# Attention and GELU layers in one kernel: x by token blocks, half of the first weights ahead of step 3's v, copies moved to ScalarE, one last store per queue

## Chip, cores, metric

One core of one Trainium2 chip (trn2). The metric is device time in microseconds (us), the median of several executions of the whole kernel. In the profiles PE is TensorE (matmuls), PEld its weight loads, DVE VectorE, ACT ScalarE, POOL GpSimd, and SP the engine that issues most transfers. Profile times count from the start of the span, which is about 2 us shorter than the device time.

## The reference

A linear attention with decay over 768 tokens in blocks of 64, for 4 sequences and 8 heads of 64, then a two-layer network with GELU on its output:

```python
intra = np.einsum('bhic,bhjc->bhij', qb, kb) * Dmask[None]
intra = np.einsum('bhij,bhjd->bhid', intra, vb)
inter = np.einsum('bhid,bhde->bhie', qb * lam_pow[None], kv_state)
out[:, :, sl] = intra + inter
kv_state = lam_block * kv_state + np.einsum('bhsd,bhse->bhde', kb_dec, vb)
# ... (cut) x = out as 3072 tokens x 512
h = x @ w_in                       # 512 x 2048
g = 0.5 * h * (1.0 + np.tanh(c * (h + 0.044715 * h * h * h)))
return g @ w_out                   # 2048 x 512
```

## The kernel before

Attention runs in 24 steps, each 256 tokens of half of the heads. A step loads q, k, v, scales them by decays (`prep`), transposes q and k (`stage_t`, called transpose n below), computes scores, masks them (`causal`), multiplies by v and by the running state (`products`), copies the result to `xT`, and updates the state (`update`: t on VectorE, u on GpSimd). Groups of 256 or 512 tokens then go through the two layers: weight blocks (`mm1`, GELU on ScalarE) and output parts (`mm2`, copied out and stored). These are kept in a list, and `fill(n)` puts n of them between attention work so that PE is never idle. For the first group the matmuls begin before x is complete.

The parts that the change touches (cut):

```python
for nm, src in (("q", q), ("k", k), ("v", v)):          # load_step(s)
    ...
for s in range(4):
    load_step(s)
for j in range(4):
    load_win(j, 2 if j == 0 else 1)                     # first weights, in two halves
# ...
if s == 2:                                              # stage_t: PSUM -> SBUF
    for hp in range(2):
        nc.scalar.activation(out=o[:, :, :, hp, :], in_=Tps[:, :, :, hp, :], func=AF.Copy)
elif s in (1, 3):
    nc.scalar.activation(out=o[:], in_=Tps[:], func=AF.Copy)
else:
    nc.vector.tensor_copy(out=o[:], in_=Tps[:])
# ...
xT[g] = xtp.tile([P, NC, len(groups[g]) * SB], FP16, ...)            # products
dst = xT[g][:, 2 * half : 2 * half + 2, i * SB : (i + 1) * SB]
# ...
def mm1_begin(f, cs):                                   # first group, before x is complete
    for c in cs:
        w = N if c < 2 else SB
        nc.tensor.matmul(first[f][:, 0:w], w_in16[:, c, f * P : (f + 1) * P], x[:, c, 0:w], ...)
# ...
for lo, hi in ((0, 384), (384, DM)):                    # the last 128 rows of the output
    # 16 matmuls, then
    nc.vector.tensor_copy(out=o32[:, lo:hi], in_=o2[:])
    for j, eng in ((0, nc.sync), (1, nc.scalar)):
        eng.dma_start(out=dst[half64(j), lo:hi], in_=o32[half64(j), lo:hi])
# ... program order, steps 1 to 3
causal(1)
update(1, 0)
update(1, 1, "t")
idle(1)
stage_t(2)
idle(3)
prep(3)
```

## Time and profile before

| | before |
|---|---|
| device time, median (range), three runs | 214.52 us (214.45 to 214.91) |
| span of the profiled run | 212.4 us, granted clock 0.996 |
| PE busy | 203.6 us, 96% |
| waits of PE after its first start | about 3 us, all before 47 us |

The page, the waits of PE and its seams are shown in the prediction below. Two more places: first, the stretch of time around transpose 2, all engines. The columns are start, duration, engine, line, operation, result and operand, count, and in brackets how long the engine had been idle and what ended that:

```profile
12.15 1.09 ACT L230 ACTIVATE qkT<-Tps 128x512 f16<-128x512 f16 x2
12.49 0.27 DVE L347 COPY t<-OK 128x128 f32<-128x128 f32 x1
...
12.88 0.61 POOL L357 TENSOR_TENSOR u<-t,lumask 128x256 f16<-128x256 f32 x1
...
13.45 1.04 POOL L204 TENSOR_TENSOR qk<-q,dq 128x512 f16<-128x512 f32 x1
...
14.56 0.62 PE L225 MATMUL Tps<-ident,qk 128*128 128x128 f16 x8 [0.40 <-POOL qk L204]
```

One sees a chain: VectorE's state t, GpSimd's u, GpSimd's q of step 3, and transpose 3 on PE waiting for that q.

Second, the end (time line, 208 us on; SPq and ACTq are issues of transfers):

```profile
208.06 1.19 SPq L416 DMA_DIRECT2D out_dram<-o  x2
208.06 1.47 ACTq L416 DMA_DIRECT2D out_dram<-o  x2
208.37 0.29 DVE L414 COPY o<-O2ps 128x128 f32<-128x128 f32 x1 [0.34 <-PE O2ps L411]
```

Each queue issues two stores of 64 partitions. The two issues that follow the last copy start at 208.74 and take 0.51 and 0.79 us. From the end of that copy (208.66) to the end of the span (212.4) it is 3.74 us; I call this the tail.

### The profile page before, as it was taken

The page shows a single profiled execution, that of the slowest core. Times are in us where ns is not written, and L with a number is a line of the kernel's source. Part 1 is how long each engine was busy: PE and PEld are TensorE (multiplying, and loading weights), DVE is VectorE, ACT ScalarE, POOL GpSimd, SP SyncE. Part 2 cuts the span into 40 slices and gives each one's busy share as a digit, 9 for nine tenths or more (in the row PEclk, how much of TensorE's full clock was granted, in tenths as well). Part 3 has the DMA queues.
Part 4 walks back from the last instruction along what each step waited for, and adds up shares of the span by engine and source line. Part 5 has one row for each costly group of instructions (what it writes and reads, how often), then busy time and mean ns, then how long its engine had stood idle before and what let it go on. Part 6 is the DMA issues. An engine that isn't in the chain of part 4 may idle for free.

```text
span 212.4 us, 5060 instructions
## 1 busy us (share of the span) xinstructions
PE 203.6 (96%) x2121; PEld 107.2 (50%) x2121; DVE 88.3 (42%) x178; ACT 94.2 (44%) x177; POOL 65.7 (31%) x82
## 2 busy tenths in 40 slices
PE   7887999989999999999999999999999999999992
PEld 2454544446865874444455455444455454444451
DVE  4885520399885623540552441452431241100111
ACT  2484764325761661677320677320666111565000
POOL 5593135356583233422412320422420110000000
PEclk9999999999999999999999999999999999999998
DMA  5999999999999999973768373714120021100122
GB/s 134 300 329 385 387 386 361 284 292 328 306 259 195 316 216 251 240 191 67 191 199 214 134 197 69 182 72 130 49 54 0 3 89 59 52 0 0 49 96 54
DMA packets 61895, 37.82 MB, mean 178 GB/s; under 512 B 17712, under 2 KB 54832, under 8 KB 61872
## 3 DMA queue, kind: packets, MB, share of 16 engines
q1 hardware_dynamic: 61712, 37.37, 63.7%
q8 instruction: 16, 0.26, 0.5%
q10 hardware_dynamic: 160, 0.13, 0.2%
q14 instruction: 7, 0.06, 0.1%
HBM read 27.27 MB, written 6.29 MB: 158 GB/s over the span
## 4 chain that ended last, share of the span: by engine, by line
PE 87%; SPq 4%; DMA 3%; DVE 3%; issue 0%; ACT 0%
PE Hps L380 37%; PE O2ps L391 36%; SPq L67 4%; DMA wi<-in_moe_w_in_dram 3%; PE Sps L255 3%; PE OK L319 3%; PE OK L310 2%; PE O2ps L411 2%; PE Hps L426 1%; PE OK L296 1%; PE Tps L225 1%; DVE o L398 1%; DVE qkT L235 1%; DVE PT L272 1%; PE Hps L432 0%
## 5 line engine op out<-in xcount | busy, mean ns | idle before, releaser
L391 PE MATMUL O2ps<-w_out,gT 128*128 128x512 f16 x368 | 83.0, 379 | 0.0
L380 PE MATMUL Hps<-xT,w_in 128*128 128x512 f16 (+1 forms) x432 | 82.5, 347 | 0.0
L382 ACT ACTIVATE gT<-Hps 128x512 f16<-128x512 f32 x92 | 54.8, 597 | 27.4 <-PE Hps L380 26.7
L380 PEld LDWEIGHTS <-w_in 128*128 128x128 f16 x432 | 41.8, 98 | 36.0
L357 POOL TENSOR_TENSOR u<-t,lumask 128x256 f16<-128x256 f32 x40 | 29.0, 732 | 90.2 <-DVE t L350 67.2
L391 PEld LDWEIGHTS <-gT 128*128 128x128 f16 x368 | 35.3, 98 | 39.5
L272 DVE TENSOR_TENSOR PT<-Sps,mask 128x1024 f16<-128x1024 f32 (+1 forms) x25 | 29.4, 1179 | 51.7 <-PE Sps L255 51.6
L327 ACT ACTIVATE xT<-OK 128x256 f16<-128x256 f32 x48 | 18.4, 452 | 56.6 <-PE OK L319 44.0
L398 DVE COPY o<-O2ps 128x512 f32<-128x512 f32 x23 | 15.8, 690 | 44.6 <-PE O2ps L391 44.5
L194 POOL TENSOR_TENSOR v<-v,dv 128x512 f16<-128x512 f32 x24 | 26.7, 1116 | 5.6 <-DMA v<-in_v_dram 3.9
L204 DVE TENSOR_TENSOR qk<-q,dq 128x512 f16<-128x512 f32 x23 | 18.0, 783 | 10.7 <-DMA q<-in_q_dram 10.6
L209 ACT ACTIVATE qk<-k 128x512 f16<-128x512 f32 x24 | 15.0, 624 | 10.5 <-DMA k<-in_k_dram 10.5
L350 DVE SCALAR_TENSOR_TENSOR t<-t,lamu,OK 128x64 f32<-128x64 f32 x64 | 14.6, 274 | 1.9 <-issue 1.1
L255 PEld LDWEIGHTS <-qkT 64*64 64x64 f16 x384 | 6.2, 106 | 10.9 <-issue 6.6
L255 PE MATMUL Sps<-qkT 64*64 64x128 f16 x384 | 10.2, 222 | 1.2 <-DVE qkT L235 0.8
L310 PE MATMUL OK<-PT,v 64*64 64x128 f16 x384 | 10.2, 218 | 0.0
L462 PE MATMUL idle<-ones 128*128 128x512 f16 x25 | 8.6, 486 | 1.5 <-DVE ones L127 1.5
L108 POOL CAST w_out<-wo 128x1024 f16<-128x1024 f32 x6 | 6.1, 1040 | 10.3 <-DMA wo<-in_moe_w_out_dram 10.3
L319 PE MATMUL OK<-qkT,u 128*128 128x128 f16 x80 | 8.8, 222 | 0.1
L310 PEld LDWEIGHTS <-v 64*64 64x64 f16 x384 | 6.7, 108 | 1.3 <-issue 1.3
L98 DVE CAST w_in<-wi 128x1024 f16<-128x1024 f32 (+1 forms) x9 | 5.5, 654 | 3.8 <-DMA wi<-in_moe_w_in_dram 3.8
L296 PE MATMUL OK<-v,qk 64*64 64x64 f16 x320 | 7.0, 192 | 0.0
(41 smaller groups left out, 60.8 us busy)
## 6 DMA issues: line engine op xcount, KB each, us to landing
q<-in_q_dram SPq DMA_DIRECT2D x24, 256.0 KB, 4.4
k<-in_k_dram SPq DMA_DIRECT2D x24, 256.0 KB, 5.1
v<-in_v_dram SPq DMA_DIRECT2D x24, 256.0 KB, 5.1
out_dram<-o SPq DMA_DIRECT2D x23, 256.0 KB, 2.7
wo<-in_moe_w_out_dram SPq DMA_DIRECT2D x4, 1024.0 KB, 14.4
wi<-in_moe_w_in_dram SPq DMA_DIRECT2D x3, 1024.0 KB, 12.2
wi<-in_moe_w_in_dram SPq DMA_DIRECT2D x2, 512.0 KB, 7.3
qkT<-qk SPq DMA_TRANSPOSE x15, 3.2
```

Source lines behind the costliest of these rows:

```text
L194: pin(nc.gpsimd.tensor_tensor(wide(tv[:]), ld32[s][2][:], decay(dv, s), ALU.mult))
L204: pin(q_eng.tensor_tensor(wide(tq), q32[:], decay(dq, s), ALU.mult))
L255: pin(nc.tensor.matmul(Sps[half64(c), hl, hp, jk, :], o[half64(hl), 1, jk, hp, half64(c)], o[half64(hl), 0, :, hp, half64(c)], start=True, ...
L272: pin(nc.vector.tensor_tensor(dst, src, mask[:].unsqueeze(1).to_broadcast([P, 4 // parts, 2 * P]), ALU.mult))
L310: pin(nc.tensor.matmul(OK[c][half64(hl), hp * P : hp * P + P], tv[half64(c), jk, 2 * hp + hl, :], PT[half64(c), hl, hp, jk, :], start=star ...
L319: pin(nc.tensor.matmul(OK[c][:, hp * P : hp * P + P], u[:, hp].rearrange("p l d -> p (l d)"), o[:, 0, :, hp, half64(c)], start=False, stop ...
L327: pin(nc.scalar.activation(out=dst[:, :, c * P : (c + 1) * P].rearrange("p hp (t j) -> p hp j t", j=2), in_=OK[c][:, 0:256].rearrange("p ( ...
L357: pin(nc.gpsimd.tensor_tensor(u[:], state[half][:].unsqueeze(2).to_broadcast([P, 2, 2, D]), lumask[:, 2 * half : 2 * half + 2, :].unsqueez ...
L380: pin(nc.tensor.matmul(Hps[:, i, :], w_in16[:, c, f * P : (f + 1) * P], x[:, c, :], start=(c == 0), stop=(c == NC - 1)))
L382: pin(nc.scalar.activation(out=gT[:, f0 : f0 + per, :], in_=Hps[:], func=AF.Gelu_apprx_tanh))
L391: pin(nc.tensor.matmul(O2[tau][:], gT[:, f, tau * P : (tau + 1) * P], w_out16[:, f, :], start=(f == 0), stop=(f == NF - 1)))
L398: pin(nc.vector.tensor_copy(out=o32[:], in_=o2[:]))
```

## The change

Its intent, in four parts. **Layout:** x is stored by token block, so that a block of a half is contiguous. **Start:** half of the first weights comes before step 3's v, transpose 2 is copied by ScalarE and VectorE together, and steps 1 to 3 are reordered. **Middle:** the first group's output copies and transposes 5 and 6 go to ScalarE, and these transposes follow the step before directly. **End:** one last store per queue. The diff, cut to its core:

```diff
-        for nm, src in (("q", q), ("k", k), ("v", v)):
+        for i, (nm, src) in enumerate((("q", q), ("k", k), ("v", v))):
+            if s == 3 and i == 2:
+                load_win(0, 0)
@@ stage_t
         if s == 2:
-            for hp in range(2):
-                pin(nc.scalar.activation(out=o[:, :, :, hp, :], in_=Tps[:, :, :, hp, :],
-                                         func=AF.Copy))
-        elif s in (1, 3):
+            pin(nc.scalar.activation(out=o[:, :, :, 0, :], in_=Tps[:, :, :, 0, :], func=AF.Copy))
+            pin(nc.vector.tensor_copy(out=o[:, :, :, 1, :], in_=Tps[:, :, :, 1, :]))
+        elif s in (1, 3, 5, 6):
@@ products
-            xT[g] = xtp.tile([P, NC, len(groups[g]) * SB], FP16, tag="xT", name=f"xT_{g}")
-        dst = xT[g][:, 2 * half : 2 * half + 2, i * SB : (i + 1) * SB]
+            xT[g] = xtp.tile([P, 2, len(groups[g]), 2, SB], FP16, tag="xT", name=f"xT_{g}")
+        dst = xT[g][:, half, i]
@@ mm1, mm1_begin, mm1_end: x[:, c, :] becomes
+        def x(c):
+            return xT[g][:, c // 2, :, c % 2, :]
@@ mm2
-            pin(nc.vector.tensor_copy(out=o32[:], in_=o2[:]))
+            if g == 0:
+                pin(nc.scalar.activation(out=o32[:], in_=o2[:], func=AF.Copy))
+            else:
+                pin(nc.vector.tensor_copy(out=o32[:], in_=o2[:]))
@@ mm2_last
-            for lo, hi in ((0, 384), (384, DM)):
+            for lo, hi, eng in ((0, 384, nc.scalar), (384, DM, nc.sync)):
...
-                for j, eng in ((0, nc.sync), (1, nc.scalar)):
-                    pin(eng.dma_start(out=dst[half64(j), lo:hi], in_=o32[half64(j), lo:hi]))
+                pin(eng.dma_start(out=dst[:, lo:hi], in_=o32[:, lo:hi]))
@@ program order, steps 1 to 3 (causal(2) is also no longer in two pieces)
     causal(1)
-    update(1, 0)
-    update(1, 1, "t")
     idle(1)
     stage_t(2)
+    update(1, 0)
     idle(3)
-    prep(3)
+    prep_qk(3)
...
     scores(3)
+    causal(3)
+    queue_group(0)
+    fill(2)
     banks = products(3, None)
     update(3, 0)
-    causal(3)
-    queue_group(0)
-    fill(4)
+    fill(2)
     products(None, 3, banks)
     cast_win(0, 0, 512, 256, c23)
+    fill(8)
+    cast_win(1)
     update(2, 1, "u")
     U(3)
-    fill(8)
@@ program order, steps 4 to 6 (the same for transpose 6)
     R(4, None)
+    stage_t(5)
     U(4)
-    fill(1)
-    stage_t(5)
     prep(6)
-    fill(1)
+    fill(2)
     R(5, 4)
```

More of the change, by code (lines that the diff above doesn't have):

```diff
@@ L74, with load_win @@
     wstage = {}
-    def load_win(j, halves=1):
-        n = NC // halves
-        t = wst.tile([P, NC, 512], FP32, tag="w32", name=f"wi32_{j}")
+    def load_win(j, part=None):
+        if not part:
+            wstage[("i", j)] = wst.tile([P, NC, 512], FP32, tag="w32", name=f"wi32_{j}")
+        t = wstage[("i", j)]
         src = moe_w_in[:, j * 512 : (j + 1) * 512].rearrange("(c p) f -> p c f", p=P)
-        for c in range(0, NC, n):
-            pin(nc.sync.dma_start(out=t[:, c : c + n, :], in_=src[:, c : c + n, :]))
-        wstage[("i", j)] = t
+        cs = slice(0, NC) if part is None else slice(2 * part, 2 * part + 2)
+        pin(nc.sync.dma_start(out=t[:, cs, :], in_=src[:, cs, :]))
     def load_wout(j):
@@ L114 @@
     for j in range(4):
-        load_win(j, 2 if j == 0 else 1)
+        load_win(j, 1 if j == 0 else None)
     for j in range(4):
@@ L259, in scores, with causal @@
         Ss[n] = Sps
-    def causal(n, parts=1):
+    def causal(n):
         t = ptp.tile([P, 2, 2, 2, P], FP16, tag="PT", name=f"PT_{n}")
-        Sps = Ss.pop(n)
-        if parts == 1:
-            pieces = [(t[:].rearrange("p a b c d -> p (a b) (c d)"),
-                       Sps[:].rearrange("p a b c d -> p (a b) (c d)"))]
-        else:
-            pieces = [(t[:, :, hp].rearrange("p a c d -> p a (c d)"),
-                       Sps[:, :, hp].rearrange("p a c d -> p a (c d)")) for hp in range(2)]
-        for dst, src in pieces:
-            pin(nc.vector.tensor_tensor(
-                dst, src, mask[:].unsqueeze(1).to_broadcast([P, 4 // parts, 2 * P]), ALU.mult))
+        pin(nc.vector.tensor_tensor(
+            t[:].rearrange("p a b c d -> p (a b) (c d)"),
+            Ss.pop(n)[:].rearrange("p a b c d -> p (a b) (c d)"),
+            mask[:].unsqueeze(1).to_broadcast([P, 4, 2 * P]), ALU.mult))
         PTs[n] = t
@@ L371, in queue_group, with by_block @@
         gT = gtp.tile([P, NF, N], FP16, tag="gT", name=f"gT_{g}")
-        x = xT[g]
         per = 512 // N
+        def x(c):
+            return xT[g][:, c // 2, :, c % 2, :]
+        def by_block(t):
+            return t.rearrange("p (b t) -> p b t", t=SB)
         def mm1(f0):
@@ L379, in mm1 @@
                 for c in range(NC):
-                    pin(nc.tensor.matmul(Hps[:, i, :], w_in16[:, c, f * P : (f + 1) * P],
-                                         x[:, c, :], start=(c == 0), stop=(c == NC - 1)))
+                    pin(nc.tensor.matmul(by_block(Hps[:, i, :]), w_in16[:, c, f * P : (f + 1) * P],
+                                         x(c), start=(c == 0), stop=(c == NC - 1)))
             pin(nc.scalar.activation(out=gT[:, f0 : f0 + per, :], in_=Hps[:],
@@ L424, in mm1_begin @@
             for c in cs:
-                w = N if c < 2 else SB
-                pin(nc.tensor.matmul(first[f][:, 0:w], w_in16[:, c, f * P : (f + 1) * P],
-                                     x[:, c, 0:w], start=(c == 0), stop=False,
+                nb = 2 if c < 2 else 1
+                pin(nc.tensor.matmul(by_block(first[f][:])[:, 0:nb], w_in16[:, c, f * P : (f + 1) * P],
+                                     x(c)[:, 0:nb], start=(c == 0), stop=False,
                                      skip_group_check=True))
@@ L432, in mm1_end @@
                 pin(nc.tensor.matmul(first[f][:, SB:N], w_in16[:, c, f * P : (f + 1) * P],
-                                     x[:, c, SB:N], start=False, stop=True,
+                                     x(c)[:, 1], start=False, stop=True,
                                      skip_group_check=True))
@@ L501 @@
     causal(1)
-    update(1, 0)
-    update(1, 1, "t")
     idle(1)
     stage_t(2)
+    update(1, 0)
     idle(3)
-    prep(3)
+    prep_qk(3)
     scores(2)
     products(2, 1)
-    causal(2, 2)
+    causal(2)
     update(2, 0)
+    prep_v(3)
     update(2, 1, "t")
@@ L514 @@
     idle(2)
-    update(1, 1, "u")
+    update(1, 1)
     products(None, 2)
@@ L520 @@
     scores(3)
+    causal(3)
+    queue_group(0)
+    fill(2)
     banks = products(3, None)
     update(3, 0)
-    causal(3)
-    queue_group(0)
-    fill(4)
+    fill(2)
     products(None, 3, banks)
     cast_win(0, 0, 512, 256, c23)
+    fill(8)
+    cast_win(1)
     update(2, 1, "u")
     U(3)
-    fill(8)
-    for j in range(1, 4):
+    for j in range(2, 4):
         cast_win(j)
@@ L544 @@
     R(4, None)
+    stage_t(5)
     U(4)
-    fill(1)
-    stage_t(5)
     prep(6)
-    fill(1)
+    fill(2)
     R(5, 4)
+    stage_t(6)
     U(5)
-    fill(1)
-    stage_t(6)
     prep(7)
-    fill(1)
+    fill(2)
     R(6, 5)
```

## The prediction

> **What bounds the kernel now.** I read the page first, then who TensorE (PE) waited for, then the time line of each engine over the first 62 us and the last 5 us, then where each DMA landed.
>
> ```profile
> PE 203.6 (96%) x2121; PEld 107.2 (50%) x2121; DVE 88.3 (42%) x178; ACT 94.2 (44%) x177; POOL 65.7 (31%) x82
> ...
> DMA  5999999999999999973768373714120021100122
> ```
>
> PE is the only engine that is nearly always busy; the DMA engines are full up to slice 18 (about 90 us). The waits of PE are few, and all lie in the first 47 us:
>
> ```profile
> PE Sps L255 <- DVE qkT L235: 0.8, 1, 0.8
> PE Hps L426 <- ACT xT L327: 0.6, 1, 0.6
> PE Hps L426 <- DVE w_in L98: 0.5, 1, 0.5
> PE Tps L225 <- DVE qk L204: 0.5, 1, 0.5
> PE Tps L225 <- POOL qk L204: 0.4, 1, 0.4
> PE Sps L255 <- ACT qkT L230: 0.2, 1, 0.2
> ```
>
> After 47 us PE never waits, so a PE that is X us early there should end X us early, if the loads keep up. These are the seams in the time lines of PE and of DVE:
>
> ```profile
> 17.47 1.90 PE L426 MATMUL Hps<-xT,w_in 128*128 128x512 f16 x8 [0.48 <-DVE w_in L98]
> 20.79 0.93 PE L426 MATMUL Hps<-xT,w_in 128*128 128x256 f16 x7 [0.63 <-ACT xT L327]
> 22.42 1.89 PE L380 MATMUL Hps<-xT,w_in 128*128 128x512 f16 x8
> ...
> 46.45 0.42 PE L255 MATMUL Sps<-qkT 64*64 64x128 f16 x16 [0.82 <-DVE qkT L235]
> ```
> ```profile
> 20.82 0.47 DVE L350 SCALAR_TENSOR_TENSOR t<-t,lamu,OK 128x64 f32<-128x64 f32 x2 [1.15 <-issue]
> 21.21 1.71 DVE L98 CAST w_in<-wi 128x1024 f16<-128x1024 f32 x2
> ...
> 42.40 1.28 DVE L398 COPY o<-O2ps 128x512 f32<-128x512 f32 x2
> 43.60 1.22 DVE L272 TENSOR_TENSOR PT<-Sps,mask 128x1024 f16<-128x1024 f32 x1
> 44.73 0.46 DVE L350 SCALAR_TENSOR_TENSOR t<-t,lamu,OK 128x64 f32<-128x64 f32 x2
> 45.11 0.68 DVE L398 COPY o<-O2ps 128x512 f32<-128x512 f32 x1
> 45.72 0.68 DVE L235 COPY qkT<-Tps 128x1024 f16<-128x1024 f16 x1
> ```
>
> The 0.63 us wait is odd: those matmuls read the first 256 tokens of step 1's half, and the copy awaited writes the second 256. In the layout by feature rows the ranges interleave, so the wait looks false. At 46.45 PE waits because DVE does four other things between 42.4 and 45.7 before it copies transpose 5.
>
> **What the Trainium skill says.** (1) "PSUM — Partial Sum Buffer", section "PSUM bank collisions raise a hardware error": no two engines may touch a bank at once, two readers included. The trace agrees: the DVE update at 20.82 sat idle 1.15 us and began as ScalarE's two copies from the same tiles (19.97 to 20.73) were done. So the two halves of transpose 2, one on ScalarE and one on VectorE from one bank, will run one after the other. (2) "ScalarE: Activation LUTs", section "What ACT_TABLE_LOAD costs": with immediates 186 ns + 0.833 ns an element, back-to-back instructions overlapping by about 93 ns. For 512 columns 612 ns; the trace has 597 (gelu) and 624 (k), and four gelus in 2.06 us. It agrees, so an output copy on ScalarE is 0.6 us, 0.52 in a row. (3) "VectorE: DVE Perf Modes", section on the TRN2 errata: from PSUM 120 + FD/Accel cycles at 0.96 GHz. For 1024 fp16 at Accel 2 that is 658 ns, the trace has 692; half of it, my estimate by this rule, is 0.39 us. (4) "DMA: Bandwidth & Descriptors", section "Issuing engines are not separate DMA queues": a second issuing engine only saves sequencer time. At the end one issue took 0.51 to 0.79 us here and the data 2.0 to 2.5 us to land; consistent.
>
> **Part 1, start to 22 us.** The queue brings q3, k3, v3 at 12.8, 13.6, 14.45 (issue plus time to landing), the first half of the first weights at 16.96 (9.94 + 7.03) and its second half at 18.3. Fifteen of the first half's sixteen shares had landed 1.2 us before the last; an instruction page of 16 KB, 1.18 us long, began at 13.7 on some engine. With the weights ahead of v3, their last share lands near k3's 13.6 + 1.3 (512 KB at 389 GB/s) + 1.2 = 16.0, and v3 takes the old place at about 16.95. Thus weights 1 us earlier, v3 2.5 us later.
>
> What feeds the first matmuls is then not the weights. DVE's half of transpose 2 follows ScalarE's (12.15 + 0.6) and ends at 13.2, as before (12.15 + 1.09). But the state copy t now comes after it, 13.2 and not 12.49. GpSimd does u before q of step 3, so q3 ends at about 15.1, not 14.49. Transpose 3 starts at 15.2 (was 14.56), its ScalarE copy ends at 16.9 (16.21), step 2's xT copies at 17.6 (17.02), and the first-weight matmuls start at 17.65 (17.47). Two blocks of four: 18.5. K products of step 3, with v3 ready at 16.95 + 1.04 = 18.0: 18.7. Two more blocks: 19.6. Step 3's products: 20.1 (xT copy began 19.97 before). Now the eight 256-column matmuls run beside the xT copies instead of behind them: 21.0. Eight ends: 21.85. The next block needs the second weight chunk, which lands at 21.0 either way; its cast now stands ahead of DVE's last update, 0.65 us: 21.65. So f=4 starts at about 21.85 instead of 22.42: **0.6 us gained**, and no more than 0.77 can be had, since the chunk's landing is fixed.
>
> **Part 2, 22 to 50 us.** Up to transpose 4 PE is solid (twelve weight blocks and nine output parts of 0.864 us each, 18.1 us), with each weight chunk cast before its use: chunks 2 and 3 at 24.65 and 27.35 against a need of 25.3 and 28.75. So transpose 4 starts at 40.0 instead of 40.55. Its k half needs k4 on ScalarE (39.48 + 0.63 = 40.11); the q half takes 0.22, so no wait. Scores 4 come at 42.25 (was 42.82). Transpose 5 now follows them directly, at 42.7, with q5 ready at 41.9 and k5 at 42.72. On ScalarE: k5 to 42.6, two output copies to 43.6, transpose 5's copy 1.02 to 44.6. PE meanwhile has 0.45 of transposes and two parts of 0.86: 44.9. The 0.82 us wait is gone; scores 5 start at 44.9 instead of 46.45: **1.55 us**. Of this 0.6 was brought along, 0.82 was the wait, the rest is rounding and mended order. Transpose 6: k6 lands at 44.6, is cast after transpose 5's copy at 45.2, PE wants it near 46.0; its copy ends at 47.7, scores 6 are due at 48.2 (was 49.70). The 1.55 holds. DVE loses 2 x 0.68 + 4 x 0.64 = 3.9 us of work between 41 and 53; that is relief, not time.
>
> **Part 3, the end.** Before, the second pair of stores was issued at 208.74 on both queues and landed by 210.94. After, 64 KB go on one queue at 208.74, and 192 KB on the other at 208.06 with somewhat longer flight. One issue less on each: 0 to 0.3, I take **0.15 us**.
>
> Sum: 0.6 + 0.95 + 0.15 = 1.7 us, 214.52 - 1.7 = **212.8 us**.
>
> **Rivals.** (a) v3 becomes the new wait. If it lands after 17.8, K products wait; each 0.5 us of it moves xT and the next block by as much, and part 1 gives 0: about 213.4. For it: v3 is at the end of a full queue. Against: 0.5 us of slack by my times. (b) ScalarE becomes the bound at 43 to 48 us: k5, outputs and two 1.02 us copies in one line. If the output copies come late or a PSUM bank is held for them, scores 5 wait 0.3 to 0.6: 213.2. Its 44% load speaks against, the tight order for. (c) Loads take the gain back: DMA is full until 90 us. Against: PE waits on no load after 45 us, and v8, the last of the first loads, lands at 50.2 while its products run at 59.8. It would make 214. (d) The matmuls that read two runs of 256 instead of one of 512 go slower: 5 groups x 64, each 10 ns would cost 3.2 us and make the kernel slower. The output stays contiguous and PE streams columns; I give it 4%. (e) The landings' lag of 1.2 us vanishes for the weights: then gains in part 1 could rise to 1.2, and 212.2.
>
> **Range and chances.** If only the 46.45 wait goes: 213.7. If all my steps hold and (e) helps: 212.1. I take 212.0 to 213.9. Faster than 2% needs 4.3 us, more than all the waits of PE after its first start (about 3 us): 0.02. Slower by 2% needs (d) at 13 ns a matmul or more: 0.01. Within 2%: 0.97.
>
> **What would show it.** In the profile after: no wait of the 256-column matmuls on xT, and f=4 at 21.7 to 22.0 (right), or a wait of K products on GpSimd's v (rival a). No wait on transpose 5's copy, scores 5 at 44.9 and scores 6 near 48.2; if PE waits there on ScalarE, rival b. First-weight matmuls at 17.5 to 17.8, not at 16.5. The 512-column matmuls still at 216 ns a piece (8 in 1.73 us). Two last stores, the end 0 to 0.3 us nearer to the last copy. It is wrong if PE's lead at 50 us is not the lead at the end, or if v3 or transpose 3 costs more than I found.

## The result, and the profile after

| | before | after |
|---|---|---|
| device time, median (range) | 214.5 us (214.45 to 214.91) | 212.67 us (212.37 to 212.75) |
| ratio | | 0.9908, 95% interval 0.9891 to 0.9925 |
| span, profiled run | 212.4 us | 210.6 us |
| VectorE / ScalarE busy | 88.3 / 94.2 us | 84.7 / 97.4 us |

Ratios here and below are the mean time of one kernel's runs over that of the other's of the same rounds, so not quite the ratio of the quoted medians. Executions over 1.5% slower than the fastest of the same kernel are left out of the means. The gain of 0.9% is clear of noise.

The total came out as predicted (212.8). The places did not. I read three marks in both traces: the first full weight block (block 4, the first matmul of `mm1` proper, called f=4), scores 6, and the start of the last two-part output.

| mark | before | after | lead |
|---|---|---|---|
| weight block 4 | 22.42 | 22.24 | 0.18 |
| scores 6 | 49.70 | 48.58 | 1.12 |
| last output's matmuls | 204.67 | 203.56 | 1.11 |
| end of the last VectorE copy | 208.66 | 207.54 | 1.12 |
| end of the span | 212.4 | 210.6 | 1.8 |

So the start gave 0.18 us, the middle 0.94, nothing was lost or won from 50 to 208 us, and the tail gave 0.68 (3.74 to 3.06). I had predicted 0.6, 0.95 and 0.15. Spans are known to 0.1 us, so a tail is good to 0.05.

The waits of PE after (engine, line, releaser, us in total, times, longest):

```profile
PE Tps L227 <- POOL qk L206: 0.7, 1, 0.7
PE Tps L227 <- DVE qk L206: 0.5, 1, 0.5
PE Sps L256 <- issue: 0.2, 1, 0.2
PE OK L314 <- POOL u L352: 0.2, 1, 0.2
...
PE Sps L256 <- DVE qkT L232: 0.2, 1, 0.2
```

The waits on xT, on the weights and on transpose 5's copy (0.6, 0.5 and 0.8 us) are gone. The wait of transpose 3 on GpSimd's q grew from 0.4 to 0.7. The stretch around transpose 2 tells why:

```profile
12.14 0.60 ACT L231 ACTIVATE qkT<-Tps 128x512 f16<-128x512 f16 x1
12.77 0.42 DVE L232 COPY qkT<-Tps 128x512 f16<-128x512 f16 x1 [0.21 <-ACT qkT L231]
...
13.11 0.28 DVE L342 COPY t<-OK 128x128 f32<-128x128 f32 x1
...
13.47 0.61 POOL L352 TENSOR_TENSOR u<-t,lumask 128x256 f16<-128x256 f32 x1 [0.52 <-DVE t L342]
14.04 1.04 POOL L206 TENSOR_TENSOR qk<-q,dq 128x512 f16<-128x512 f32 x1
```

VectorE's half sat idle until ScalarE's half had ended, though both only read the bank. The two halves also interleave in the tile that they write, as x did; but scores' first eight matmuls read one half from 12.79, while VectorE was still writing the other (12.77 to 13.19), so the interleaving made nobody wait there. The same split over two banks was not run. The second half is ready no earlier than before (scores' second half at 13.25, was 13.28), but t, u and q each moved back by 0.6 us, and transpose 3 starts at 15.14 instead of 14.56. PE's seams after:

```profile
17.70 1.04 PE L429 MATMUL Hps<-xT,w_in 128*128 128x512 f16 x4
...
20.49 1.04 PE L429 MATMUL Hps<-xT,w_in 128*128 128x256 f16 x8
21.37 1.03 PE L435 MATMUL Hps<-xT,w_in 128*128 128x256 f16 x8
22.24 10.52 PE L381 MATMUL Hps<-xT,w_in 128*128 128x512 f16 x48
...
45.38 0.42 PE L256 MATMUL Sps<-qkT 64*64 64x128 f16 x16
```

From 17.70 to 22.24 PE has work without a pause, and scores 5 start without any bracket, so without a wait. The 48 full matmuls take 10.52 us in both traces: reading two runs of 256 instead of one of 512 costs nothing. The end after:

```profile
206.95 0.37 ACTq L419 DMA_DIRECT2D out_dram<-o  x1
207.25 0.29 DVE L418 COPY o<-O2ps 128x128 f32<-128x128 f32 x1 [0.34 <-PE O2ps L415]
207.57 0.33 SPq L419 DMA_DIRECT2D out_dram<-o  x1
```

An issue now takes 0.33 to 0.37 us, and from issue to landing it is 1.6 to 1.9 us (before: 2.0 to 2.5).

### The profile page after: what moved, and what is told of

It is laid out like the page before. It is cut to its first block, busy times and chain, and to the rows that moved or that the text cites. A ratio compares the mean times of both kernels' runs of the same rounds, so it can differ in the third digit from the quotient of the medians.

```text
span 210.6 us, 5057 instructions
## 1 busy us (share of the span) xinstructions
PE 203.4 (97%) x2121; PEld 107.0 (51%) x2121; DVE 84.7 (40%) x172; ACT 97.4 (46%) x182; POOL 65.6 (31%) x82
## 4 chain that ended last, share of the span: by engine, by line
PE 91%; POOL 3%; DMA 2%; SPq 1%; issue 1%; DVE 0%; POOLq 0%
PE Hps L381 38%; PE O2ps L392 38%; PE Sps L256 4%; PE OK L314 3%; PE OK L305 3%; DMA v<-in_v_dram 2%; PE O2ps L415 2%; PE Tps L227 1%; PE Hps L429 1%; SPq L69 1%; PE OK L291 1%; POOL u L352 1%; POOL v L196 1%; POOL qk L206 0%; PE Hps L435 0%
## 5 line engine op out<-in xcount | busy, mean ns | idle before, releaser
L352 POOL TENSOR_TENSOR u<-t,lumask 128x256 f16<-128x256 f32 x40 | 29.8, 751 | 89.1 <-DVE t L345 64.8
L265 DVE TENSOR_TENSOR PT<-Sps,mask 128x1024 f16<-128x1024 f32 x24 | 29.4, 1224 | 56.0 <-PE Sps L256 55.9
L402 DVE COPY o<-O2ps 128x512 f32<-128x512 f32 x19 | 13.1, 691 | 44.6 <-PE O2ps L392 44.5
L196 POOL TENSOR_TENSOR v<-v,dv 128x512 f16<-128x512 f32 x24 | 25.8, 1077 | 6.9 <-DMA v<-in_v_dram 6.9
L206 DVE TENSOR_TENSOR qk<-q,dq 128x512 f16<-128x512 f32 x23 | 17.3, 752 | 10.6 <-DMA q<-in_q_dram 10.6
L465 PE MATMUL idle<-ones 128*128 128x512 f16 x25 | 8.0, 459 | 1.5 <-DVE ones L129 1.5
L227 PE MATMUL Tps<-ident,qk 128*128 128x128 f16 x72 | 5.9, 220 | 1.5 <-POOL qk L206 0.7
```

Source lines behind the costliest of these rows:

```text
L196: pin(nc.gpsimd.tensor_tensor(wide(tv[:]), ld32[s][2][:], decay(dv, s), ALU.mult))
L206: pin(q_eng.tensor_tensor(wide(tq), q32[:], decay(dq, s), ALU.mult))
L265: pin(nc.vector.tensor_tensor(t[:].rearrange("p a b c d -> p (a b) (c d)"), Ss.pop(n)[:].rearrange("p a b c d -> p (a b) (c d)"), mask[:]. ...
L352: pin(nc.gpsimd.tensor_tensor(u[:], state[half][:].unsqueeze(2).to_broadcast([P, 2, 2, D]), lumask[:, 2 * half : 2 * half + 2, :].unsqueez ...
```

## The experiments

The total was right by two errors that cancelled, so the question was which part does what. Theory: the parts add; the tail gains by the shape of the stores, the middle by relief of VectorE, and the start loses by its new order most of what the layout gives. Rival: the tail's 0.5 us is chance, and the start is held by something else (the late v, or the weights). Twelve kernels ran, all correct, each timed in five rounds against the kernel before. Marks from the profiles (one execution each; a blank is a mark that was not needed there), device times as medians of four to six runs:

| kernel | transpose 2 | transpose 3 | block 4 | transpose 4 to scores 6 | tail | time | ratio to before (95%) |
|---|---|---|---|---|---|---|---|
| before | 11.49 | 14.56 | 22.42 | 9.15 | 3.74 | 214.5 | 1 |
| after | 11.49 | 15.14 | 22.24 | 8.21 | 3.06 | 212.67 | 0.9908 (0.9891 to 0.9925) |
| e1 stores | 11.39 | 14.43 | 22.46 | 9.15 | 3.00 | 213.73 | 0.9962 (0.9947 to 0.9978) |
| e2 middle | 11.70 | 14.78 | 22.64 | 8.21 | 3.76 | 213.43 | 0.9949 (0.9935 to 0.9963) |
| e3 start | 11.71 | 15.37 | 22.38 | 9.15 | 3.69 | 214.21 | 0.9993 (0.9975 to 1.001) |
| e4 layout | 11.97 | 15.06 | 22.12 | 9.15 | 3.73 | 213.97 | 0.9974 (0.9959 to 0.9988) |
| e12 after again | 11.93 | 15.59 | 22.59 | | 3.01 | 212.67 | 0.9923 (0.9911 to 0.9935) |
| e6 q early | 11.73 | 14.77 | 22.49 | | 3.05 | 212.61 | 0.9917 (0.9902 to 0.9931) |
| e11 layout, middle, stores | 12.24 | 15.31 | 22.27 | 8.21 | 3.03 | 212.21 | 0.9896 (0.9883 to 0.9909) |
| e5 v first | 12.26 | 15.92 | 22.93 | | 3.07 | 212.63 | 0.9915 (0.9902 to 0.9928) |
| e8 | | | | 8.21 | 2.95 | 212.73 | 0.9918 (0.9905 to 0.993) |
| e9 | | | | 8.21 | 3.52 | 213.12 | 0.9936 (0.9923 to 0.9949) |
| e13 best | 11.96 | 15.04 | 22.14 | | 3.03 | 212.28 | 0.9895 (0.988 to 0.9911) |
| e14 split | 11.66 | 15.31 | 22.31 | | 2.98 | 212.72 | 0.9916 (0.9902 to 0.9929) |

The first column shows an offset of up to 0.9 us from run to run in the first steps, so I compare distances between marks.

**e1: the last stores alone**, on the kernel before.

```diff
-            for lo, hi in ((0, 384), (384, DM)):
+            for lo, hi, eng in ((0, 384, nc.scalar), (384, DM, nc.sync)):
-                for j, eng in ((0, nc.sync), (1, nc.scalar)):
-                    pin(eng.dma_start(out=dst[half64(j), lo:hi], in_=o32[half64(j), lo:hi]))
+                pin(eng.dma_start(out=dst[:, lo:hi], in_=o32[:, lo:hi]))
```

> The kernel before with only its last stores changed: one per queue, all 128 partitions each. Theory (traces): the tail from the end of the last VectorE copy to the end of the span, 3.73 us before, becomes 3.06 as in the changed kernel, and nothing else moves: span 211.7, ratio 0.997. Rival (my prediction): one issue less saves 0.15 us only: span 212.25; the other half us of the shorter tail would then belong to chance.

Measured: tail 3.00, span 211.7, ratio 0.9962. The theory holds and my 0.15 us is refuted. The tail is 3.69 to 3.76 in all four kernels with the old stores and 2.95 to 3.07 in all eight with one store for each of the two pieces, so it is not chance.

**e2: the middle alone.** Output copies of the first group and transposes 5 and 6 on ScalarE, with the new order of steps 4 to 6.

```diff
-        elif s in (1, 3):
+        elif s in (1, 3, 5, 6):
-            pin(nc.vector.tensor_copy(out=o32[:], in_=o2[:]))
+            (ScalarE if g == 0, else VectorE)
     R(4, None)
+    stage_t(5)
     U(4)
-    fill(1)
-    stage_t(5)
     prep(6)
-    fill(1)
+    fill(2)
```

> The kernel before with only the middle changed: group 0's output copies and transposes 5 and 6 on ScalarE, and transposes 5 and 6 placed right behind the step before. Theory: the start up to transpose 4 stays (40.55), the 0.82 us wait of scores 5 goes and 0.1 us of drift with it: scores 5 at 45.55, scores 6 at 48.75 against 49.70; span shorter by 0.95. Rival: without the earlier start ScalarE is no later than before relative to PE, so a longer gain of 1.0 to 1.1, or ScalarE's line of k, two outputs and a 1.02 us copy makes scores 5 wait and the gain is below 0.6.

Measured: from transpose 4 to scores 6 it is 8.21 us against 9.15, a gain of 0.94 us, with no wait of PE in the stretch. The theory holds to 0.01 us; that run's start was 0.2 us late, so its marks are later than named. Ratio 0.9949.

**e3: the start alone** (with the layout): the changed kernel with last stores, output copies, transposes 5 and 6 and the order of steps 4 to 6 put back.

> The changed kernel with the last stores and the middle put back: only x by blocks, the early half of the weights and the new order of steps 1 to 3. Theory: f=4 at 22.24 and transpose 4 at 40.37 as in the changed kernel, then the 0.8 us wait of scores 5 on VectorE again; span shorter by 0.18, time ratio 0.999. Rival: the 0.18 us is lost at the wait, because VectorE's line at 42 to 46 us depends on loads and not on PE: no gain at all.

Measured: block 4 at 22.38, the 0.81 us wait at scores 5 again, ratio 0.9993. By time it can't be told from no gain; the mark is 0.04 us earlier than before's. Theory and rival differ too little here to be separated. Added up, the three parts give 0.9962 + 0.9949 + 0.9993 - 2 = 0.9904, and the changed kernel has 0.9908 and 0.9923: the parts add.

**e4: the layout alone.**

```diff
-            xT[g] = xtp.tile([P, NC, len(groups[g]) * SB], FP16, tag="xT", name=f"xT_{g}")
-        dst = xT[g][:, 2 * half : 2 * half + 2, i * SB : (i + 1) * SB]
+            xT[g] = xtp.tile([P, 2, len(groups[g]), 2, SB], FP16, tag="xT", name=f"xT_{g}")
+        dst = xT[g][:, half, i]
```

> The kernel before with only x laid out by token blocks. Theory: the false wait of 0.63 us on the copies of step 3 goes, the eight 256-column matmuls run beside the copies, and f=4 starts at 21.8 instead of 22.42, later than the cast of the second weight chunk allows (second chunk lands at 21.0; its cast stands behind VectorE's update, which waits for the copies' end at 20.8, so the cast ends at 21.9): f=4 at 21.9, span shorter by 0.5. So layout alone would do better in this stage than the whole start part did (0.18). Rival: the matmuls with two runs of 256 are slower (twelve blocks of four would take more than 10.36 us), or the cast ends later than 22.2 and f=4 waits for it, so a gain under 0.25.

Measured on PE:

```profile
20.05 1.04 PE L431 MATMUL Hps<-xT,w_in 128*128 128x256 f16 x8
20.95 1.03 PE L437 MATMUL Hps<-xT,w_in 128*128 128x256 f16 x8
22.12 2.12 PE L385 MATMUL Hps<-xT,w_in 128*128 128x512 f16 x9
```

The wait on xT is gone: the 256-column matmuls run as one row of eight, so the wait was false and the layout cures it. Block 4 comes at 22.12, although this run began 0.5 us late (transpose 2 at 11.97). The eight last 256-column matmuls take 0.87 us, so PE was ready at about 21.8 and stood 0.3 us until the cast of the second weight chunk. Ratio 0.9974: the layout alone gives more than the whole start part (0.9993). The intervals overlap a little; that the rest of the start costs is settled by e11 below.

**e12: the changed kernel again**, as the yardstick.

> The changed kernel itself, unaltered, as the yardstick for the three that follow on the same chip. All theories: ratio to before 0.991 (0.9908 measured), about 212.6, f=4 between 22.1 and 22.3 when transpose 3 starts at 15.1.

Measured: 0.9923, block 4 at 22.59 with transpose 3 at 15.59: 7.00 us apart, against 7.10 in the first run.

**e6: GpSimd's q early** in the changed kernel (cut).

```diff
-            pin(nc.scalar.activation(out=o[:, :, :, 0, :], in_=Tps[:, :, :, 0, :], func=AF.Copy))
-            pin(nc.vector.tensor_copy(out=o[:, :, :, 1, :], in_=Tps[:, :, :, 1, :]))
+            (both halves on ScalarE)
     causal(1)
+    update(1, 0)
+    update(1, 1, "t")
     idle(1)
     stage_t(2)
-    update(1, 0)
```

> The changed kernel with transpose 2 copied by ScalarE alone and step 1's two state updates back ahead of it, so that GpSimd does q of step 3 as early as in the kernel before. Theory: GpSimd's late q is what sets the start: transpose 3 comes 0.6 us earlier (14.5 instead of 15.1), the first-weight matmuls at 17.1 instead of 17.7, then K products of step 3 wait for v (18.3) by 0.2 to 0.3 or not, f=4 at 21.8 to 22.0; faster than the changed kernel by 0.25 to 0.45 us. Rival: the late v of step 3 sets it (landing at 17.1 to 17.2, decayed at 18.3), so an earlier transpose 3 turns into a wait on v and nothing is gained (less than 0.1).

Measured: 212.61 against 212.67, ratio 0.9917 against 0.9923: no clear gain, so my theory's number failed here (the intervals overlap widely, so a gain of 0.2 us is not excluded). Transpose 3 did come 0.6 us earlier (3.04 us after transpose 2, not 3.66). But PE then stopped elsewhere:

```profile
16.51 0.41 PE L257 MATMUL Sps<-qkT 64*64 64x128 f16 x14
17.77 0.24 PE L257 MATMUL Sps<-qkT 64*64 64x128 f16 x2 [0.85 <-issue]
```

In the middle of 16 like matmuls PE stood for 0.85 us, and no engine released it. The changed kernel has a shorter stop of 0.24 us at the same instruction. The rival, the late v, had no part in that stop: K products (of k and v, for the state), which need v, come after the first of the first-weight matmuls. An instruction page of 16 KB was in transfer from 15.04 to 16.17 here (14.86 to 16.04 in the changed kernel's run). The packed traces of all fourteen profiles fit it: in six (e6, the changed kernel, e8, e14, e9, e2) the fifteenth of these sixteen matmuls starts 0.08 to 1.07 us after the fourteenth, and always 1.34 to 1.61 us after that page's end. In the other eight the two start together, and the page had ended 1.37 us or more before. So a late instruction page is the likely cause; no run moved the page on purpose, so it is not shown.

**e11: layout, middle and stores, without the rest of the start**, on the kernel before (e4, e2 and e1 together).

> The kernel before with layout, middle and last stores, but not the early half of the weights nor the new order of steps 1 to 3. If the parts add (0.9974 + 0.9949 + 0.9962 - 2): ratio 0.9885, about 212.0, that is 0.6 us faster than the changed kernel, f=4 at 21.9 to 22.1. Rival: middle and layout overlap (the middle's gain was measured with the 0.6 us wait in place) or the layout's gain was the run's offset: ratio 0.991, equal to the changed kernel.

Measured: 212.21 us, ratio 0.9896, against 0.9923 for the changed kernel on the same chip; the intervals do not overlap. The interval (0.9883 to 0.9909) holds the sum, 0.9885, and not the rival's 0.991. It is faster than both kernels. Block 4:

```profile
21.09 1.03 PE L439 MATMUL Hps<-xT,w_in 128*128 128x256 f16 x8
22.27 1.90 PE L385 MATMUL Hps<-xT,w_in 128*128 128x512 f16 x8
```

PE is done with the 256-column matmuls at 21.96 and waits 0.31 us for the cast. This although transpose 2 came 0.75 us later than in the two kernels' profiled runs: here the cast of the second weight chunk sets block 4, not PE. The chunk had landed at 21.17, and its cast stood behind VectorE's update until 21.52.

**e5: v of step 3 first again** in the changed kernel.

```diff
-            if s == 3 and i == 2:
-                load_win(0, 0)
     for j in range(4):
+        if j == 0:
+            load_win(0, 0)
         load_win(j, 1 if j == 0 else None)
```

> The changed kernel with the first half of the first weights loaded after v of step 3 again, all else kept. Theory (GpSimd's late q sets the start, so weights at 15.0 or 17.0 make little difference): first-weight matmuls at 17.5 to 17.7, v ready at 16.1, f=4 within 0.1 of the changed kernel's, same time within 0.15 us. Rival: the early weights are what feeds the first matmuls: their start moves to 18.1 or later and the kernel loses 0.4 us.

Measured: 212.63 against 212.67. From transpose 2 to block 4 it is 10.67 us, against 10.66 in the changed kernel. The mark itself is at 22.93 because the run began late, so the theory's "within 0.1" holds for the distance and not for the mark. The early weights are worth nothing in this order.

**e8: output copies on VectorE, and both last stores on one queue**, two edits of the changed kernel that are read at two places.

```diff
-            if g == 0:
-                pin(nc.scalar.activation(out=o32[:], in_=o2[:], func=AF.Copy))
-            else:
-                pin(nc.vector.tensor_copy(out=o32[:], in_=o2[:]))
+            pin(nc.vector.tensor_copy(out=o32[:], in_=o2[:]))
-            for lo, hi, eng in ((0, 384, nc.scalar), (384, DM, nc.sync)):
+            for lo, hi, eng in ((0, 384, nc.sync), (384, DM, nc.sync)):
```

> The changed kernel with two separate edits, read at two places: group 0's output copies back on VectorE (read at scores 5 and 6), and both last stores on one queue (read from the end of the last VectorE copy to the end of the span). Middle, theory: moving transposes 5 and 6 alone removes the 0.8 us wait, for VectorE then has only the copies and the mask; scores 5 without a wait. Rival: the masked scores of step 4, behind two output copies on VectorE, come late and PE waits 0.3 or more in steps 5 or 6. Tail, theory: the first store was issued 0.6 us earlier, so the second does not collide on one queue: 3.06 us as in the changed kernel. Rival: the second queue is what the shorter tail needs: 3.4 or more.

Measured: transpose 4 to scores 6 8.21 us, tail 2.95. Both theories hold: the output copies need not move, and the second queue is not needed.

**e9: transposes 5 and 6 on VectorE, and the very last store in two halves**, again read at two places.

```diff
-        elif s in (1, 3, 5, 6):
+        elif s in (1, 3):
-                pin(eng.dma_start(out=dst[:, lo:hi], in_=o32[:, lo:hi]))
+                h = P // len(engs)     # one engine for 384 columns, two for the last 128
+                for j, eng in enumerate(engs):
+                    pin(eng.dma_start(out=dst[j * h : (j + 1) * h, lo:hi],
+                                      in_=o32[j * h : (j + 1) * h, lo:hi]))
```

> The changed kernel with two separate edits, read at two places: transposes 5 and 6 copied by VectorE again (output copies stay on ScalarE), and the very last 128 columns stored as two halves of 64 partitions on the two queues at once, while the 384 columns stay one store. Middle, theory: transpose 5 then waits for the mask and update of step 4 (to 44.7), its copy ends at 45.3 where scores 5 are due at 45.4: no wait over 0.2, so either move alone would have done. Rival: VectorE is late and scores 5 wait 0.5 or more. Tail, theory: two issues at the same moment of 64 partitions each are what cost: issues of 0.5 to 0.8 us instead of 0.33 and a tail of 3.6 to 3.75. Rival: only the number of stores ahead counts: 3.1.

Measured: transpose 4 to scores 6 8.21 us again, so with the new order either move alone removes the wait. Whether the new order alone would do, with both left on VectorE, was not run. The tail is 3.52:

```profile
207.19 1.18 ACTq L421 DMA_DIRECT2D out_dram<-o  x2
207.49 0.29 DVE L418 COPY o<-O2ps 128x128 f32<-128x128 f32 x1 [0.34 <-PE O2ps L415]
207.81 0.56 SPq L421 DMA_DIRECT2D out_dram<-o  x1
```

The two halves start together at 207.81, and both issues take 0.56 us instead of 0.33. Most of the old tail is back with one halved store (0.5 of the 0.7 us). It is a little under the 3.6 that I named. Whether it is the half height or the simultaneous issue was not separated.

**e13: e11, with the cast of the second chunk ahead of VectorE's last update.**

> Layout, middle and stores on the kernel before, and in addition the cast of the second weight chunk ahead of VectorE's last update of step 3 (as the changed kernel has it). Theory: f=4, at 22.27 in the run without it and held 0.3 us by that cast, comes at 21.9 to 22.0; ratio 0.988 to 0.989, the fastest of all. Rival: the second chunk's landing moves with the instruction page and takes it back: 0.9896 as without.

Measured: 0.9895 against 0.9896; block 4 at 22.14, held by a cast that started at 21.39, when the chunk had landed. The rival holds: the landing (21.37, against 21.17 in e11) sets this mark, which comes only 0.13 us earlier, and the time is the same.

**e14: e11 with transpose 2 split as in the changed kernel.**

```diff
     causal(1)
-    update(1, 0)
-    update(1, 1, "t")
     idle(1)
-    stage_t(2)     # both halves on ScalarE
+    stage_t(2)     # ScalarE and VectorE
+    update(1, 0)
+    update(1, 1, "t")
```

> Layout, middle and stores on the kernel before, with transpose 2 split between ScalarE and VectorE and step 1's updates behind it, as in the changed kernel; no early weights. Theory: VectorE's half starts only when ScalarE's has ended, so scores 2 come no earlier, while GpSimd's u and q of step 3 come 0.6 us later, so transpose 3 and the start of the first-weight matmuls slip by 0.3 to 0.6 and the kernel loses 0.3 us or more against the same without it (0.9896): about 0.991. Rival: the late q is hidden by the wait for the weights (17.1 landing): no loss over 0.1, and then the early weights or the late v cost the changed kernel its start.

Measured: transpose 3 comes 3.65 us after transpose 2, against 3.07 in e11 and 3.08 in e13; the edit costs 0.58 us at that point. By time 212.72 (212.4 to 212.81) against 212.28 (212.14 to 212.38) for e13. The four runs of each do not overlap, though the intervals of the ratios overlap and e13 also has its cast moved. In the profiled runs block 4 and the span are equal (22.31 and 22.27; 210.6 both), because that run of e14 began 0.6 us earlier than e11's. So the edit uses up 0.6 us of slack on PE, and it probably costs 0.4 us in the mean of the runs.

The edit moves two things, the split and the place of the updates behind it. In the trace of the kernel before, t of this step was done at 12.76, and VectorE's half began at 12.77 in the changed kernel; with t left ahead of it, the split would hardly have delayed GpSimd. So it looks like the order that costs, not the split as such; that was not run. Nor were the other moves of the start (the mask of step 2 in one piece, v of step 3 scaled later, the new order of the fills) run alone.

## Why the prediction was right or wrong

The total (1.7 us predicted, 1.83 by medians) was right; of its three terms one was exact and two were mis-sized in opposite directions, so that the total came so close is luck.

- **Part 1, the start: mis-sized, 0.6 predicted, 0.18 measured.** The chain was right nearly to its end. VectorE's half does follow ScalarE's, transpose 3 starts at 15.14 (15.2 predicted), and the first-weight matmuls at 17.70 (17.65). The step that failed is the sum after that: I took 4.2 us from there to block 4, and it is 4.54. Blocks in twos take 0.96 us each time, not 0.85 and 0.9, K products 0.26, not 0.2, and step 3's products 0.61, not 0.5. Splitting eight matmuls of 512 in two fours cost about 0.1 us: eight in a row took 1.83 before, two fours 1.92. The cast at 21.17 would have allowed 21.8.
- **The landings in part 1: half right.** v3 landed at 17.2 (16.95 predicted) and the early weights at 15.0, not 16.0. (The trace shows sixteen completions for each load, its shares.) The instruction page that I placed at 13.7, and that the trace of the kernel before has from 13.47, began at 14.86 and hit v's last share instead. Neither number mattered (e5).
- **Part 2: right.** 0.95 predicted, 0.94 measured in both the changed kernel and e2. Scores 6 came at 48.58 and not at 48.2 only by what part 1 had lost.
- **Part 3: mis-sized, 0.15 predicted, 0.68 measured.** The step that failed: I counted one issue less, and took its cost for the whole gain. What counted is that two stores of 64 partitions issued together take 0.5 to 0.8 us to issue and 2.0 to 2.5 us to land, against 0.33 and 1.6 to 1.9 us for whole stores. I read the 0.51 and 0.79 us as the price of an issue, though an ordinary store just ahead of them, at 205.59, took 0.33. e1, e8 and e9 show it.
- **The rivals.** (a) v3 did not become a wait: it was scaled at 18.27, and its products were due at 18.66. (b) ScalarE did not bind: transpose 5's copy ended at 44.85, and scores 5 came at 45.38. (c) The loads took nothing back: the lead is 1.12 at 49 us and at 208 us. (d) Two runs of 256 cost nothing. (e) The weights did land without the lag, and it did not help.

## What to carry to other kernels

Two readers of one PSUM bank took turns here (VectorE idle for 0.21 us until ScalarE was done), so splitting a copy between two engines saved nothing, and the updates put behind the second copy came 0.6 us later. A wait between ranges that do not overlap can be one of layout; make what is written at a time contiguous, and test that alone before reordering around it (e4 gained more than the whole start part, e11 more than the whole change). At the end of a kernel store each piece whole over all partitions, and read the length of an issue against one that stands alone.

## What the Trainium skill lacked or had wrong

- "DMA: Bandwidth & Descriptors": the section "Issuing engines are not separate DMA queues" says that a second issuing engine saves only sequencer time, and the page's rules for kernel authors already prefer one transfer of 128 partitions to two of partition halves. The runs agree. What the page lacks is the price at a kernel's end: issues of 0.51 to 0.79 us for 64-partition stores issued together against 0.33 to 0.38 us for whole ones, and a tail of 3.52 to 3.76 us against about 3.0. Both whole stores on one queue did as well (2.95).
- "VectorE: DVE Perf Modes", section on the TRN2 errata: the PSUM rule gives 392 and 658 ns for 512 and 1024 fp16 columns; measured 425 and 692 ns, some 34 ns more in both.
- "ScalarE: Activation LUTs", section "What ACT_TABLE_LOAD costs": it gives one fixed term for every source. For 512 columns its 612 ns lies between the measured 590 ns (output copy from PSUM) and 624 ns (k from SBUF). The errata table of the VectorE page does tell the two sources apart.
- "Runtime: NRT & Kernel Launch", section "Instruction fetch mechanics": it calls the cost of crossing a 16 KiB block "mostly hidden". In these runs a page of 16 KB, moved as one packet, took 1.05 to 1.21 us, and in the changed kernel the last of v3's sixteen shares landed 1.34 us after the fifteenth; PE's stops at one matmul (0.85 us in e6) fit such pages, though that they come from them is not shown.
- No page tells of the offset of up to 0.9 us between executions in the first 12 us (transpose 2 at 11.39 to 12.26). In e1 and e5, its two ends, GpSimd's first v starts at 6.42 and 7.32, in e5 after 1.42 us of waiting for its load, so the first loads land at different times.
